# Attention into SwiGLU on one core: regrouping the feed-forward work and re-pricing the planner

## The chip, the cores and the metric

One core of a Trainium2 chip runs the whole program. The metric is the device time of one execution in microseconds, lower is better; the time before is the median of three runs.

## The reference

Attention with a threshold on 8 batches of 8 heads, 576 rows and 64 columns per head, and a SwiGLU feed-forward on the 4608 rows that come out of it.

```
scores = (1/8) * q @ k.T                       # per batch and head, 576 x 576
thresh = max(scores, axis=-1) - tau            # tau = 0.02
scores = where(scores >= thresh, scores, -1e9)
attn   = softmax(scores);  o = attn @ v        # 576 x 64 per head
x  = o of all heads side by side               # 4608 x 512
xn = x / sqrt(mean(x*x) + 1e-6) * rms_g
out = (silu(xn @ w_gate) * (xn @ w_val)) @ w_out   # 512 -> 1536 -> 512
```

## The kernel before

The 4608 rows are cut into 36 **chunks** of 128 rows. A chunk `("m", b, c)` holds 128 of the first 512 rows of batch b; a chunk `("v", i, 0)` holds the last 64 rows of batch 2i and of batch 2i+1. The order of the chunks is: four "m" of batch 0, one "v", four "m" of batch 1, four of batch 2, "v", and so on. A chunk takes four **steps**, one for each pair of heads, so there are 144 steps, numbered 0 to 143 here.

A step s does the following.

- A **score burst** on PE (`emit_s`, L377, or L389 for "v" chunks): queries against keys in fp32, two heads on the two halves of the array, into the two PSUM tiles `s_ps`. The next burst needs both tiles read.
- DVE reads them (L410: scale, copy to `ssb`, running minimum to `mx`), POOL adds tau (L417, `nth`), and ACT (L428, L435, L432, L447) with POOL (L461, L466) makes the thresholded weights `wsb`.
- The weights are transposed to `wt`: in the first 16 steps (`N_PE`) by PE (L480) and two DVE copies (L488), later by a DMA on SP's queue (L494).
- PE multiplies them by v (`emit_av`, L511, or L516 for "v" chunks) into `ot`; after two steps DVE divides by the row sums (L537, L538) into `xsb`.

After four steps the chunk is normalized (`emit_x`: ACT L549, POOL L552, L554, L557) and transposed by a DMA on SP (L561) into its place in `xnT[slot]`.

Chunks are put together in **groups** of 1, 2 or 4 (128, 256 or 512 rows) for the feed-forward (`emit_ffn`). For each of 12 slices of the 1536 columns PE does a gate burst of four matmuls (L600) and a value burst of four (L605) into the PSUM `ring`; ACT takes tanh (L614), DVE forms silu (L617) and the product (L622). Then for each chunk an output burst of 12 matmuls (L641), an ACT copy (L647) and a store. A group can start when its last chunk has been transposed.

The program order on each engine is not written by hand. Every piece of work is an `Op` with an engine, an estimated cost in ns (`COST`), dependencies and a priority in units of steps; `order_ops` is a list scheduler that runs through estimated time, always takes the operation that can start first, and among those that can start at the same time the one with the lowest priority number. The result is the order in which each engine's instructions are issued, and on the chip each engine takes them in that order. Feed-forward operations have the priority (step of the group's last chunk + a lag), spread over `pace` steps for each 512 rows (`st`, `dt` and `clock` in `emit_ffn`).

Loads and stores come from SP's queue, loads of v and `w_out` from POOL's. The weights are cast by DVE (L699) as they arrive in the first hundred microseconds.

Of the kernel before, what the change touches and what calls it, by code (L numbers as in the profile page):

```python
# [11 lines left out]
ALU = mybir.AluOpType  # L12

SEM = 160.0
COST = dict(
    s_main=1120.0, s_virt=1130.0, tr4=480.0, tr8=560.0, av_main=360.0, av_virt=500.0, ffn4=216.0,
    ttr=690.0, evac_qk=600.0, evac_kt=350.0, prelu=700.0, exp2=1250.0, exp1=690.0, exp0=690.0,
    mask_d=750.0, mask_g=1740.0, take_g=1300.0,
    trw=560.0, evac_w=420.0, rz=180.0, xmul=400.0, sq=800.0, xn=750.0, pool_tiny=270.0, pool_mean=800.0, pool_dma=800.0, sp=70.0,
# [15 lines left out]
def order_ops(ops, ring_sizes):  # L35


    import heapq

    ring_free = {r: [(0.0, i) for i in range(n)] for r, n in ring_sizes.items()}  # L40
    users = {}
    left = {}
    for i, o in enumerate(ops):
        left[i] = len(o.deps)
        for d in o.deps:
            users.setdefault(id(d), []).append(i)
    pending = {}
    for i, o in enumerate(ops):
        pending.setdefault(o.eng, [])
        if not left[i]:  # L50
            pending[o.eng].append(i)
    eng_free = {e: 0.0 for e in pending}
    dma_free = 0.0
    out = []
    ready_at = {i: 0.0 for i in range(len(ops))}
    while len(out) < len(ops):
        best = None
        for e, lst in pending.items():
            if not lst:
                continue  # L60
            t0 = eng_free[e]
            cand = None
            for i in lst:
                o = ops[i]
                t = max(t0, ready_at[i])
                if o.ring is not None:
                    if len(ring_free[o.ring]) < o.nring:
                        continue
                    t = max(t, sorted(ring_free[o.ring])[o.nring - 1][0])
                k = (t, o.prio, i)  # L70
                if cand is None or k < cand:
                    cand = k
            if cand is not None and (best is None or cand < best[0]):
                best = (cand, e)
        (t, _, i), e = best
        o = ops[i]
        o.start = t
        if o.ring is not None:
            o.slot = []
            for _ in range(o.nring):  # L80
                got = min(ring_free[o.ring])
                ring_free[o.ring].remove(got)
                o.slot.append(got[1])
        eng_free[e] = t + o.cost
        if o.dma:
            dma_free = max(dma_free, t + o.cost) + o.dma
            o.end = max(dma_free, t + o.cost) + 2000.0
        else:
            o.end = t + o.cost
        if o.frees is not None:  # L90
            ring_free["R"].append((o.end + SEM, o.frees[0].slot[o.frees[1]]))
        for slot in o.opens:
            ring_free["R"].append((o.end + SEM, slot))
        pending[e].remove(i)
        out.append(o)
        for j in users.get(id(o), []):
            u = ops[j]
            ready_at[j] = max(ready_at[j], o.end + (0.0 if u.eng == o.eng and not o.dma else SEM))
            left[j] -= 1
            if not left[j]:  # L100
                pending[u.eng].append(j)
    return out
# [3 lines left out]
def kernel(  # L106
# [13 lines left out]
    B, H, S, D = q.shape  # L120
# [51 lines left out]
    NXT = 3  # L172
# [22 lines left out]
    def add(eng, cost, prio, deps, fn, **kw):  # L195
        o = Op(eng, cost, prio, deps, fn, **kw)
        ops.append(o)
        return o


    chunks = []
# [44 lines left out]
    def emit_qk(b, p, prio):  # L246
# [14 lines left out]
        for j in (1, 0):  # L261
# [4 lines left out]

            t = add("PE", COST["tr4"], prio, [los[1 - j], o_id] + last_s.get(("k", b - 2, p), []), tr, ring="R")

# [6 lines left out]

            done.append(add(EVAC[j], COST["evac_qk"], prio, [t], ev, frees=(t, 0)))
        tr_of.append(t)
# [12 lines left out]
    def emit_k_tail(b, prio):  # L290
# [9 lines left out]
        deps = [x for p in range(NP) for x in last_s.get(("k", b - 2, p), [])]  # L300
        t = add("PE", COST["tr4"], prio, [tail_load["k", b], o_id] + deps, tr, ring="R")

        def ev(o):
            nc.scalar.copy(out=kTt[b % 2], in_=ring[t.slot[0]][:, 0:64 * NP].rearrange("p (a n) -> p a n", n=TAIL))

        kt_ready[b] = add("ACT", COST["evac_kt"], prio, [t], ev, frees=(t, 0))
        tail_load.setdefault(("use", i), []).append(t)

    def emit_q_tail(i, prio):
        def tr(o):  # L310
            for p in range(NP):
# [35 lines left out]
    def emit_batch_inputs(b):  # L347
        base = first_step[b - 1] if b else -10
        emit_tail_load(b, base + (4 if b else 1))
        for p in range(NP):  # L350
            pr = base + 3.3 * p + 3 if b else -10 + p
            emit_qk(b, p, pr)
            if p == 0:
                emit_k_tail(b, pr + (2 if b else 0.2))
        emit_v(b, base + 5 if b else -1)
        if b % 2:
            emit_q_tail(b // 2, base + 14.5)
# [305 lines left out]


    ci_of = {c: i for i, c in enumerate(chunks)}
    groups = [[("m", 0, 0), ("m", 0, 1)], [("m", 0, 2), ("m", 0, 3)]]
    for i in range(B // 2):
        if i:
            groups.append([("m", 2 * i, c) for c in range(4)])
        if i % 2:  # L670
            groups.append([("v", i - 1, 0), ("v", i, 0)])
        if 2 * i + 1 < B - 1:
            groups.append([("m", 2 * i + 1, c) for c in range(4)])
    groups += [[("m", B - 1, 0), ("m", B - 1, 1)], [("m", B - 1, 2)], [("m", B - 1, 3)]]
    place, last_of = {}, {}
    for gi, g in enumerate(groups):
        for j, c in enumerate(g):
# [2 lines left out]
    xt_op = {}  # L680
# [7 lines left out]
    n = 0  # L688
# [21 lines left out]
    for j in range(4):  # L710
        o = add("POOL", COST["pool_dma"], W_FROM + W_STEP * n + j, [], lambda o, j=j: nc.gpsimd.dma_start(
            out=wo[:, 3 * j:3 * j + 3], in_=wo_src[:, 3 * j:3 * j + 3]), dma=3000.0)
        wo_ld.append(gated(o, W_FROM + W_STEP * n + j))

    for s, (ci, p) in enumerate(steps):
        kind, b, c = chunks[ci]
        so = s_of[s] = emit_s(s)
        emit_softmax(s, so)
        emit_av(s)
        if p % 2:  # L720
            emit_half(s)
        if p == NP - 1:
            gi, j = place[ci]
            xt_op[ci] = emit_x(ci, s, gi % NXT, 128 * j)
            if ci in last_of:
                g = groups[last_of[ci]]
                emit_ffn(last_of[ci] % NXT, [(ci_of[x], xt_op[ci_of[x]]) for x in g], s + 5, PACE)
            if kind == "v" and 2 * b + 2 < B:
                emit_batch_inputs(2 * b + 2)
            if kind == "m" and b % 2 and c == 3 and b + 2 < B:  # L730
                emit_batch_inputs(b + 2)
# [11 lines left out]
            o.fn(o)  # L743


PACE = 16.0
FIRST = 0
WAYS = ("pg", "pp")
NSTAGE = 4
# [43 lines left out]
```

## Time and profile before

| what | value |
|---|---|
| runs | 639.76, 640.0, 643.23 us; median 640.0 |
| the profiled execution | 637.34 us, of which the span from the first to the last instruction is 635.6 us |
| PE busy | 602.6 us (95%) |
| ACT, DVE, POOL busy | 461.5 us (73%), 441.3 us (69%), 382.3 us (60%) |
| mean granted PE clock | 0.986 |
| bytes moved by DMA | 84.29 MB, 133 GB/s on average |

Busy time of PE counts the pipeline's latency of each burst, so that 95% busy doesn't say that no time is lost; how much work a stretch holds is worked out in the prediction from the distances between starts of bursts that follow each other without a wait.

### The profile page before, as it was taken

The page shows a single profiled execution, that of the slowest core. Times are in us where ns is not written, and L with a number is a line of the kernel's source. Part 1 is how long each engine was busy: PE and PEld are TensorE (multiplying, and loading weights), DVE is VectorE, ACT ScalarE, POOL GpSimd, SP SyncE. Part 2 cuts the span into 40 slices and gives each one's busy share as a digit, 9 for nine tenths or more (in the row PEclk, how much of TensorE's full clock was granted, in tenths as well). Part 3 has the DMA queues.
Part 4 walks back from the last instruction along what each step waited for, and adds up shares of the span by engine and source line. Part 5 has one row for each costly group of instructions (what it writes and reads, how often), then busy time and mean ns, then how long its engine had stood idle before and what let it go on. Part 6 is the DMA issues. An engine that isn't in the chain of part 4 may idle for free.

```text
span 635.6 us, 13838 instructions
## 1 busy us (share of the span) xinstructions
PE 602.6 (95%) x5008; PEld 362.5 (57%) x5008; DVE 441.3 (69%) x1129; ACT 461.5 (73%) x741; POOL 382.3 (60%) x518
## 2 busy tenths in 40 slices
PE   5799979997999999999999999999999999998996
PEld 3566756764645545555765445555555444556774
DVE  3799976756578758865868765886587658856653
ACT  2778857687776878977977777987687877876332
POOL 4799565758495745966785654876396744653000
PEclk9999979999799999999999999999999999999999
DMA  9999876887798556987896549997797553445100
GB/s 167 163 186 175 163 169 116 145 164 125 146 142 119 105 149 138 146 141 152 175 170 121 87 94 185 150 152 134 181 145 133 104 142 82 94 118 117 42 34 35
DMA packets 296725, 84.29 MB, mean 133 GB/s; under 512 B 287440, under 2 KB 288976, under 8 KB 296656
## 3 DMA queue, kind: packets, MB, share of 16 engines
q1 hardware_dynamic: 256400, 77.11, 57.8%
q0 software_dynamic: 40256, 6.30, 13.5%
q8 instruction: 39, 0.64, 0.4%
q14 instruction: 30, 0.25, 0.2%
HBM read 37.75 MB, written 9.44 MB: 74 GB/s over the span
## 4 chain that ended last, share of the span: by engine, by line
PE 79%; DVE 8%; DMA 4%; issue 3%; POOL 3%; ACT 2%; SPq 0%; DVEq 0%; POOLq 0%; ACTq 0%
PE s_ps L377 24%; PE ring L641 12%; PE ring L605 12%; PE ring L600 12%; PE ot L511 6%; PE ring L264 4%; DVE ssb L410 3%; DMA wt<-wsb 3%; PE s_ps L389 2%; PE s_ps L641 2%; PE ot L516 1%; POOL wsb L461 1%; DVE sl L617 1%; DVE hf L622 1%; PE s_ps L600 1%
## 5 line engine op out<-in xcount | busy, mean ns | idle before, releaser
L410 DVE CUSTOM_DVE_ANT_0 ssb<-s_ps,zrow 128x576 f32<-128x576 f32 x288 | 209.5, 753 | 104.1 <-PE s_ps L377 72.3
L428 ACT ACTIVATE ssb<-ssb,nth 128x576 f32<-128x576 f32 x216 | 159.1, 765 | 49.0 <-POOL nth L417 48.4
L377 PE MATMUL s_ps<-qkT 64*128 64x512 f32 x512 | 172.4, 658 | 8.2 <-DVE mx L410 5.7
L461 POOL TENSOR_SCALAR wsb<-ssb,nth 128x576 f16<-128x576 f32 x72 | 124.9, 1735 | 9.4 <-PE ring L480 3.7
L417 POOL TENSOR_SCALAR nth<-mx 128x2 f32<-128x2 f32 x144 | 32.1, 223 | 152.6 <-DVE mx L410 131.1
L605 PE MATMUL ring<-xnT,wv 128*128 128x512 f16 (+2 forms) x520 | 106.9, 328 | 2.1 <-DVE sl L617 2.1
L600 PE MATMUL ring<-xnT,wg 128*128 128x512 f16 (+2 forms) x524 | 107.4, 327 | 0.0
L377 PEld LDWEIGHTS s_ps<-kTt,qkT 64*128 64x128 f32 x512 | 63.8, 192 | 57.2 <-issue 54.9
L466 POOL TENSOR_TENSOR wsb<-wsb,esb 128x576 f16<-128x576 f16 x72 | 92.3, 1281 | 5.6
L614 ACT ACTIVATE th<-ring 128x512 f32<-128x512 f32 (+2 forms) x131 | 63.4, 488 | 35.9 <-PE ring L600 33.2
L435 ACT ACTIVATE wsb<-ssb 128x1152 f16<-128x1152 f32 x72 | 83.7, 1162 | 4.8 <-DMA wt<-wsb 1.5
L617 DVE SCALAR_TENSOR_TENSOR sl<-th,ring 128x512 f32<-128x512 f32 (+2 forms) x131 | 72.3, 552 | 17.8 <-ACT th L614 17.6
L641 PE MATMUL ring<-wo,hf 128*128 128x512 f16 x372 | 84.7, 379 | 0.0
L622 DVE TENSOR_TENSOR hf<-ring,sl 128x512 f16<-128x512 f32 (+2 forms) x130 | 72.9, 561 | 10.7 <-PE ring L605 1.1
L333 POOL DMA_DIRECT2D va<-in_v_dram x112 | 77.2, 694 | 2.7 <-PE s_ps L377 0.6
L377 PEld LDWEIGHTS s_ps<-qkT 64*128 64x128 f32 x512 | 51.1, 189 | 46.9 <-DVE mx L410 24.6
L600 PEld LDWEIGHTS <-wg 128*128 128x128 f16 x624 | 54.6, 98 | 31.8 <-issue 0.5
L605 PEld LDWEIGHTS <-wv 128*128 128x128 f16 x624 | 53.5, 97 | 32.4 <-issue 4.2
L511 PE MATMUL ot<-va,wt 128*128 128x65 f16 x1280 | 62.0, 195 | 5.8 <-DMA wt<-wsb 4.9
L641 PEld LDWEIGHTS <-hf 128*128 128x128 f16 x432 | 40.6, 98 | 47.1 <-issue 1.9
L447 ACT ACTIVATE esb<-ssb,nth 128x576 f16<-128x576 f32 x72 | 55.4, 770 | 15.7 <-POOL nth L417 15.5
L511 PEld LDWEIGHTS <-wt 128*128 128x128 f16 x1280 | 53.1, 98 | 19.3 <-DMA wt<-wsb 6.2
(53 smaller groups left out, 574.6 us busy)
## 6 DMA issues: line engine op xcount, KB each, us to landing
qkn<-in_k_dram SPq DMA_DIRECT2D x64, 128.0 KB, 3.5
qkn<-in_q_dram SPq DMA_DIRECT2D x64, 128.0 KB, 3.4
out_dram<-osb SPq DMA_DIRECT2D x32, 256.0 KB, 2.6
stage<-in_moe_w_gate_dram SPq DMA_DIRECT2D x12, 256.0 KB, 3.2
stage<-in_moe_w_val_dram SPq DMA_DIRECT2D x12, 256.0 KB, 3.5
va<-in_v_dram POOLq DMA_DIRECT2D x80, 32.0 KB, 3.6
va<-in_v_dram POOLq DMA_DIRECT2D x32, 64.0 KB, 4.0
wt<-wsb SPq DMA_TRANSPOSE x128, 3.2
```

What stands on the lines that cost most here:

```text
L377: nc.tensor.matmul(s_ps[h][:, lo:lo + n], qkT[b % 2][p][hs, c], src[hs], start=True, stop=True)
L410: nc.vector.tensor_tensor_reduce(out=ssb[a][:, h], in0=s_ps[h][:, 448:1024], in1=zrow, scale=-1.0 / 8.0, scalar=3.0e38, op0=ALU.add, op1=A ...
L428: nc.scalar.activation(out=ssb[a][:, h], in_=ssb[a][:, h], func=PRELU, scale=-1.0, bias=nth[m][:, h:h + 1], **PRELU_KW)
L435: nc.scalar.activation(out=wsb[s % NW], in_=ssb[a], func=AF.Exp)
L461: nc.gpsimd.tensor_scalar(out=wsb[s % NW][:, h], in0=ssb[a][:, h], scalar1=nth[m][:, h:h + 1], scalar2=None, op0=ALU.is_le)
L466: nc.gpsimd.tensor_tensor(out=wsb[s % NW][:, h], in0=wsb[s % NW][:, h], in1=esb[es], op=ALU.mult)
L511: nc.tensor.matmul(ot[:, cs], w[:, 4 * h + j], va[b % 2][:, p, 5 * h + j], start=(j == 0), stop=(j == 4))
L600: nc.tensor.matmul(ring[o.slot[0]][:, 0:n], wg[d][:, fs], xnT[slot][:, d, 0:n], start=(d == 0), stop=(d == 3))
L605: nc.tensor.matmul(ring[o.slot[0]][:, 0:n], wv[d][:, fs], xnT[slot][:, d, 0:n], start=(d == 0), stop=(d == 3))
L617: nc.vector.scalar_tensor_tensor(out=sl[i][:, 0:n], in0=th[i][:, 0:n], scalar=1.0, in1=ring[g.slot[0]][:, 0:n], op0=ALU.add, op1=ALU.mult)
L622: nc.vector.tensor_tensor(out=hf[hi][:, 0:n], in0=ring[vv.slot[0]][:, 0:n], in1=sl[i][:, 0:n], op=ALU.mult)
L641: nc.tensor.matmul(ring[o.slot[0]], hf[hs[fc][0]][:, 128 * j:128 * (j + 1)], wo[:, fc], start=(fc == 0), stop=(fc == NFC - 1))
```

## The change

The groups are now made of consecutive chunks of either kind, in the sizes 2, 2, 2, 2, then six of 4, then 2, 1, 1. Before they were, in chunks: (0,1), (2,3), (5-8), (9-12), (4,13), (14-17), (18-21), (23-26), (27-30), (22,31), (32,33), (34), (35); now they are (0,1), (2,3), (4,5), (6,7), (8-11), (12-15), (16-19), (20-23), (24-27), (28-31), (32,33), (34), (35). Both have six groups of 4, five of 2 and two of 1. The lag in the priority of a group goes from 5 to 10 steps, the pace from 16 to 13 steps for 512 rows. The estimated cost of a score burst goes from 1120 to 1260 ns ("m") and from 1130 to 1250 ns ("v"). `SLACK` is 0, so that the new line in `order_ops` gives what the old one gave.

```diff
+SLACK = 0.0
 COST = dict(
-    s_main=1120.0, s_virt=1130.0, tr4=480.0, ...
+    s_main=1260.0, s_virt=1250.0, tr4=480.0, ...
...
-            ready_at[j] = max(ready_at[j], o.end + (0.0 if u.eng == o.eng and not o.dma else SEM))
+            wait = 0.0 if u.eng == o.eng and not o.dma else SEM + (SLACK if u.eng == "PE" else 0.0)
+            ready_at[j] = max(ready_at[j], o.end + wait)
...
-    groups = [[("m", 0, 0), ("m", 0, 1)], [("m", 0, 2), ("m", 0, 3)]]
-    for i in range(B // 2):
-        if i:
-            groups.append([("m", 2 * i, c) for c in range(4)])
-        if i % 2:
-            groups.append([("v", i - 1, 0), ("v", i, 0)])
-        if 2 * i + 1 < B - 1:
-            groups.append([("m", 2 * i + 1, c) for c in range(4)])
-    groups += [[("m", B - 1, 0), ("m", B - 1, 1)], [("m", B - 1, 2)], [("m", B - 1, 3)]]
+    groups, at = [], 0
+    for n in SIZES:
+        groups.append(chunks[at:at + n])
+        at += n
+    assert at == len(chunks)
...
-                emit_ffn(last_of[ci] % NXT, [(ci_of[x], xt_op[ci_of[x]]) for x in g], s + 5, PACE)
+                emit_ffn(last_of[ci] % NXT, [(ci_of[x], xt_op[ci_of[x]]) for x in g], s + LAG, PACE)
...
-PACE = 16.0
+PACE = 13.0
+SIZES = (2, 2, 2, 2, 4, 4, 4, 4, 4, 4, 2, 1, 1)
+LAG = 10.0
```

The instructions on each engine are the same in kind, shape and number; only their order moves (lines of the changed kernel from `order_ops` on are two higher, weight casts two lower). Three places show it.

**PE, step 36** (`s_ps` is the score tile, `wt` a transposed weight tile, `ot` its product with v, `wv` and `wg` the value and gate weights). Before, the burst is followed by the first of ten matmuls against v:

```order
L377 MATMUL s_ps_172<-qkT_0_82 128x512
L377 MATMUL s_ps_173<-qkT_0_82 128x512
L377 MATMUL s_ps_172<-kTt_90,qkT_0_82 128x64
L377 MATMUL s_ps_173<-kTt_90,qkT_0_82 128x64
L511 LDWEIGHTS wt_120
L511 MATMUL ot<-va_95,wt_120 128x65
```

In the changed kernel the same burst is followed by a value burst, a gate burst and another value burst of a group of 256 rows, and only then by the matmuls against v:

```order
L379 MATMUL s_ps_172<-qkT_0_82 128x512
L379 MATMUL s_ps_173<-qkT_0_82 128x512
L379 MATMUL s_ps_172<-kTt_90,qkT_0_82 128x64
L379 MATMUL s_ps_173<-kTt_90,qkT_0_82 128x64
L607 LDWEIGHTS wv_70
L607 MATMUL ring_176<-xnT_141,wv_70 128x256
L607 LDWEIGHTS wv_71
L607 MATMUL ring_176<-xnT_141,wv_71 128x256
```

Before, steps 32 to 40 hold no feed-forward burst at all; now each of them holds one to four.

**ACT, steps 50 to 52** (`ssb` scores, `wsb` weights, `th` tanh of a gate burst, `osb` an output row block, `xsq` the sum of squares that starts a chunk's normalization). Before:

```order
L614 ACTIVATE th_144<-ring_175 128x512
L428 ACTIVATE ssb_96<-ssb_96,nth_108 128x576 x2
L435 ACTIVATE wsb_114<-ssb_96 128x1152
L447 ACTIVATE esb_113<-ssb_97,nth_109 128x576
L647 ACTIVATE osb_170<-ring_176 128x512
L428 ACTIVATE ssb_97<-ssb_97,nth_109 128x576
L432 ACTIVATE wsb_115<-ssb_97 128x576
L647 ACTIVATE osb_171<-ring_175 128x512
```

Now:

```order
L649 ACTIVATE osb_171<-ring_177 128x512
L274 COPY qkT_3_89<-ring_175 128x512
L551 ACTIVATE xsq_127,ssq_130<-xsb_126 128x512
L323 COPY qTv_93<-ring_176 128x512
L449 ACTIVATE esb_112<-ssb_98,nth_107 128x576
L430 ACTIVATE ssb_98<-ssb_98,nth_107 128x576
L434 ACTIVATE wsb_116<-ssb_98 128x576
L430 ACTIVATE ssb_96<-ssb_96,nth_108 128x576 x2
L437 ACTIVATE wsb_114<-ssb_96 128x1152
```

Before, a tanh and output blocks of a group stand among the weights of these steps; now the last output block of group (6,7) is copied ahead of them, and the first tanh of group (8-11) comes after three more rows.

**DVE, steps 17 to 19** (L410 reads the scores of a step, L488 copies transposed weights of an earlier step). Before:

```order
L410 ISA ssb_97,mx_100<-s_ps_172,zrow 128x576
L410 ISA mx_100 128x1
L488 COPY wt_121<-ring_177 128x640
L488 COPY wt_121<-ring_175 128x512
L410 ISA ssb_97,mx_100<-s_ps_173,zrow 128x576
L410 ISA mx_100 128x1
L488 COPY wt_117<-ring_176 128x640
L488 COPY wt_117<-ring_177 128x512
```

Now:

```order
L490 COPY wt_121<-ring_176 128x640
L490 COPY wt_121<-ring_175 128x512
L624 TENSOR_TENSOR hf_153<-ring_177,sl_145 128x256
L412 ISA ssb_96,mx_99<-s_ps_172,zrow 128x576
L412 ISA mx_99 128x1
L412 ISA ssb_96,mx_99<-s_ps_173,zrow 128x576
L412 ISA mx_99 128x1
L490 COPY wt_117<-ring_176 128x640
L490 COPY wt_117<-ring_175 128x512
```

The transposed weights of steps 14 and 15 were copied during and after the scores of step 19 (`ssb_97`, `mx_100`); now they are copied before and after those of step 18 (`ssb_96`, `mx_99`).

More of the change, by code (lines that the diff above doesn't have):

```diff
@@ L14 @@
 SEM = 160.0
+SLACK = 0.0
 COST = dict(
-    s_main=1120.0, s_virt=1130.0, tr4=480.0, tr8=560.0, av_main=360.0, av_virt=500.0, ffn4=216.0,
+    s_main=1260.0, s_virt=1250.0, tr4=480.0, tr8=560.0, av_main=360.0, av_virt=500.0, ffn4=216.0,
     ttr=690.0, evac_qk=600.0, evac_kt=350.0, prelu=700.0, exp2=1250.0, exp1=690.0, exp0=690.0,
```

## The prediction

> **What bounds the kernel now.** I read the page first (engine shares and slices), then the windows, then one line's windows, PE's timeline and the waits. On the page:
>
> ```profile
> span 635.6 us, 13838 instructions
> ...
> PE 602.6 (95%) x5008; PEld 362.5 (57%) x5008; DVE 441.3 (69%) x1129; ACT 461.5 (73%) x741; POOL 382.3 (60%) x518
> ...
> PE   5799979997999999999999999999999999998996
> ...
> PEclk9999979999799999999999999999999999999999
> ```
>
> PE is the bound from about 200 us on. The slices that are not full, and the two in which the granted clock dips, lie before. The windows, cut where score bursts 0, 16, 24, 32, 48 and the last one start (columns: stretch, length, then busy time of PE, PEld, DVE, ACT, POOL, then granted clock, DMA share and GB/s):
>
> ```profile
> 9.60:65.50 55.90, 50.53 (x433) 34.50 (x433) 46.97 (x121) 39.70 (x58) 44.35 (x59) 1.00 0.99 178
> 65.50:99.60 34.10, 30.01 (x281) 20.66 (x280) 27.42 (x73) 21.97 (x39) 17.69 (x23) 0.90 0.76 160
> 99.60:141.60 42.00, 41.79 (x395) 28.81 (x394) 27.69 (x78) 32.28 (x58) 27.42 (x36) 1.00 0.80 143
> 141.60:202.20 60.60, 53.88 (x386) 32.44 (x384) 39.75 (x99) 43.74 (x67) 42.62 (x59) 0.92 0.87 135
> 202.20:576.50 374.30, 372.39 (x3024) 206.22 (x3023) 264.41 (x648) 298.89 (x460) 237.98 (x321) 1.00 0.71 134
> 576.50:635.60 59.10, 51.18 (x488) 37.87 (x488) 32.74 (x104) 22.98 (x62) 6.15 (x9) 1.00 0.20 52
> ```
>
> PE's busy time includes latency, so I price its work by distances between starts where nothing waits:
>
> ```profile
> 119.40 0.61 PE L605 MATMUL ring<-xnT,wv 128*128 128x256 f16 x4
> 119.85 0.60 PE L600 MATMUL ring<-xnT,wg 128*128 128x256 f16 x4
> 120.28 0.60 PE L605 MATMUL ring<-xnT,wv 128*128 128x256 f16 x4
> ...
> 218.34 5.18 PE ring L641 x24
> ...
> 390.09 1.02 PE ring L264 x8
> ...
> 404.04 1.13 PE L377 MATMUL s_ps<-qkT 64*128 64x512 f32 x4
> 405.00 0.34 PE L377 MATMUL s_ps<-kTt,qkT 64*128 64x64 f32 x4
> 405.27 1.04 PE L600 MATMUL ring<-xnT,wg 128*128 128x512 f16 x4
> 406.15 0.48 PE L511 MATMUL ot<-va,wt 128*128 128x65 f16 x10
> 406.47 1.02 PE L605 MATMUL ring<-xnT,wv 128*128 128x512 f16 x4
> 407.33 1.03 PE L600 MATMUL ring<-xnT,wg 128*128 128x512 f16 x4
> 408.29 1.13 PE L377 MATMUL s_ps<-qkT 64*128 64x512 f32 x4
> ```
>
> A score burst takes 1.23 us (404.04 to 405.27), a gate or value burst 0.86 at 512 rows and 0.44 at 256, a burst against v 0.32, an output burst 5.18/2 = 2.59, a pair of q and k transposes 1.0. Switching into a score burst costs 0.10 (0.96 against 0.86). With these prices I add up PE's work in any stretch of the program, by counting bursts in the two orders. Over the whole program both come to 560 us; the other 75 us of the span are PE without work, and only they can change.
>
> **Steps 32 to 47, the main term.** The feed-forward gate bursts and the score bursts by stretch (PE, PEld):
>
> ```profile
> 99.60:141.60 42.00, 9.03 (x60) 5.55 (x60) 1.00 0.80 143
> 141.60:166.90 25.30, 0.00 (x0) 0.00 (x0) 0.81 0.86 144
> 166.90:202.20 35.30, 9.20 (x36) 3.29 (x36) 0.99 0.88 129
> ...
> 141.60:166.90 25.30, 15.41 (x65) 9.21 (x65) 0.81 0.86 144
> ```
>
> The first three rows are L600, the last L377. From 141.6 to 166.9 there is no gate burst: group (5-8) has to wait for chunk 8. A score burst has 8 records, so 65 are 8.1 bursts, 3.1 us each, while PE had about 1.8 us of work per step. Here the softmax sets the pace. For steps 32 to 47 before: 16 score bursts (19.7), 15 against v (4.8), 4 pairs of transposes (4.0), 17 feed-forward bursts at 512 rows (14.6) and switches (1.3) make 44.4 us in 60.6 us, 16.2 without work. In the changed order the same steps carry 47 feed-forward bursts at 256 rows (20.7), 4 output bursts (10.4) and one more burst against v: 61.1 us. The idle time is filled with work that is taken from stretches where PE is full (6.4 us from steps 24 to 31, 2.7 from the tail, the rest from later steps), and those shorten by as much. Some idle time remains. Steps 24 to 31, where the order already alternates score and feed-forward bursts of 256 rows, hold 40.5 us of work in 42.0, so 1.5 in 8 steps; I take 3.0 in 16 steps. Gain 13.2; ends: 16.2 (nothing is left idle) and 8.
>
> The clock belongs to this term: 0.81 granted from 141.6 to 166.9, 1.00 where PE is fed. [...]
>
> **Steps 16 to 23.** 34.1 us hold 22.2 us of work before and 21.5 now, at a clock of 0.90. Steps 20 to 22 had no feed-forward burst; now steps 20 and 21 have four and three, of group (0,1), which is running there in both. But DVE, which also casts the weights here, was busy for 27.42 us and does the same work, so the gain is at most 34.1 - 27.4 = 6.7; at worst the same waits return behind other bursts (loss 1). I take 2, nearer to the row of DVE than to none, because DVE waits between its own instructions too.
>
> **Steps 0 to 15.** Work and pieces are the same, but the burst against v now follows three score bursts after its own in steps 5 to 13, where it followed four (six in step 13), and the later score bursts stand behind it in PE's order. Step 8:
>
> ```profile
> 38.42 1.52 PE L377 MATMUL s_ps<-qkT 64*128 64x512 f32 x4
> ...
> 54.08 0.48 PE L511 MATMUL ot<-va,wt 128*128 128x65 f16 x10
> ...
> 32.00:64.00 32.00, 30.58 (x260) 19.90 (x260) 31.02 (x80) 24.75 (x37) 29.82 (x41) 1.00 0.92 178
> ```
>
> That is 15.7 us from its score burst to its burst against v. If this latency stayed, steps would come every 15.7/4 = 3.9 us and not every 3.4 (55.9/16 = 3.5), a loss of about 5 over nine steps. But DVE is at 31.02 of 32 us here: most of the latency is queueing, which shrinks when fewer steps are in flight. I take a loss of 1; ends: gain 1, loss 5.
>
> **Steps 50 to 56: the new dry stretch.** Group (6,7) ends at step 49 with two output bursts, and group (8-11) cannot start before chunk 11 is normalized. Steps 50 to 56 hold 16.9 us of PE work in the new order (29.8 before, inside the full stretch from 202.2): 7 score bursts (8.4), 6 feed-forward bursts (5.2), the rest against v. At the 3.1 us per step seen without feed-forward work they would take 21.7, a loss of 4.8; if the softmax has caught up during the output bursts, none. Before the first gate burst stands 5.2 us of PE work from chunk 11's last burst against v; what has to happen meanwhile is
>
> ```profile
> L538 DVE TENSOR_TENSOR xsb<-ot,rz 128x256 f32<-128x256 f32 x72 | 30.6, 425 | 5.2 <-POOL xn L557 2.7
> L549 ACT ACTIVATE xsq<-xsb 128x512 f16<-128x512 f32 x36 | 22.3, 620 | 2.7 <-DVE xsb L538 2.6
> L554 POOL TENSOR_TENSOR ir<-irm,mhalf 128x1 f32<-128x1 f32 x36 | 21.0, 582 | 3.0
> L557 POOL TENSOR_SCALAR xn<-xsb,ir 128x512 f16<-128x512 f32 x36 | 25.1, 698 | 3.6
> ...
> xnT<-xn SPq DMA_TRANSPOSE x36, 2.5
> ```
>
> 0.4 + 0.6 + 0.6 + 0.7 + 2.5 = 4.8 us and a wait between each two, so the gate burst is late by some 2 us. I take a loss of 3.
>
> **The rest.** From step 57 to the last score burst both orders alternate in the same way and PE is full (372.39 of 374.30): no change, give or take 1. The tail from the last score burst has the same last groups (2, 1, 1); its work goes from 47.8 to 45.1 us (counted above), and its idle time of 11.3 us mostly lies in the groups of one chunk and the last store. The burst against v of step 143 now stands behind two output bursts and will wait less: gain 0.5, ends -1 and 1.5. Grouping, lag, pace and the two costs act through the order alone; `SLACK` of 0 does nothing. Cross-kind groups cost nothing extra on PE: the tail of "v" chunks is stored by the same two DMAs as before, on SP's queue.
>
> **Sum.** 13.2 + 2 - 1 - 3 + 0.5 = 11.7 us. The span falls from 635.6 to 623.9, the profiled execution from 637.3 to 625.6. That execution was 2.7 us below the median of the runs; against the median the forecast is 640.0 - 11.7 = 628.3 us.
>
> **Rivals.** (a) The idle time of steps 32 to 47 is due to the transposing DMAs, not to missing work, and stays.
>
> ```profile
> 151.46 4.29 DMA wt<-wsb
> ...
> 179.57 6.93 DMA wt<-wsb
> ...
> PE ot L511 <- DMA wt<-wsb: 3.2, 3, 2.0
> DVE ssb L410 <- PE s_ps L377: 17.2, 15, 2.5
> ```
>
> For it: those two pieces of the chain, with a DMA share of 0.87. Against it: PE waited for them 3.2 us in three waits, and DVE waited 17.2 us for scores, so the loop was short of PE's order and not of transposes alone; and now 10 to 17 us of work stand between a score burst and its burst against v in steps 32 to 47, where there were 6 to 10 in steps 32 to 39. If 8 more of the 16.2 us stay: 636. [...]
>
> (b) Slower: the shorter reach in steps 5 to 20. If the latencies stay as they were (15.7 us in step 8, and more after step 12 while weights are cast), each burst against v holds back the score burst after the next three. Chaining them by the new order puts step 28 some 16 us later; with 13.2 + 2 - 3 + 0.5 gained elsewhere this gives 643, and it decides the sign from about 13 us of loss. Against it: DVE's 97% says that the queue, not the reach, set the pace.
>
> (c) More is won: nothing remains idle in steps 32 to 47, steps 16 to 23 gain 5, the dry stretch costs nothing: 640.0 - 22 = 618, between 616 and 622.
>
> (d) The reordering moves idle time without removing it, since the work is equal: within 3 us of 640.
>
> **Chances.** Forecast (622 to 633) 0.64, (c) 0.12, (a) 0.13 (633 to 639), (d) 0.06, (b) 0.05. The bound between a change and none is 0.5%, 3.2 us, which is also about what runs of this kernel can tell. Faster takes the forecast, (c) and half of (a): 0.83; same the other half and most of (d): 0.11; slower (b) and a little of (d): 0.06. The range leaves out (b), (d) and half of (c): 619 to 637.
>
> **What would show it.** Right: the granted clock at 1.00 from step 24 on, steps 32 to 47 taking about 64 us with gate bursts throughout, some 3 us of idle PE near step 52, the tail after the last score burst near 56 us. Wrong: PE waiting for transposes or for `mx` in steps 32 to 47, step 16 starting clearly later than 65.5 us, or new idle time of over 5 us after step 57.

## The result, and the profile after

The changed kernel takes 622.96 us (median of four runs, 620.76 to 625.11). The kernel before, in runs beside it, takes 639.88. The ratio is 0.973 with a 95% interval of 0.967 to 0.979, a gain of 16.9 us where 11.7 were forecast. The profiled execution took 620.76 us.

The page of the changed kernel, the lines that answer to those of before:

```profile
span 619.0 us, 13823 instructions
...
PE 592.0 (96%) x5008; PEld 354.8 (57%) x5008; DVE 439.2 (71%) x1129; ACT 460.0 (74%) x741; POOL 383.6 (62%) x518
...
PE   5798999999999999999999999999999999999996
...
PEclk9999999999999999999999999999999999999999
```

Both dips of the granted clock are gone in this execution, and of the gaps in PE's row only those of the first 60 us and of the end are left. The windows of the changed kernel, cut at the same six places (starts of score bursts 0, 16, 24, 32, 48 and 143; columns as before):

```profile
9.30:68.40 59.10, 51.73 (x452) 35.13 (x452) 48.97 (x127) 40.39 (x60) 45.32 (x60) 1.00 0.98 180
68.40:96.80 28.40, 25.73 (x277) 17.55 (x276) 23.78 (x66) 21.79 (x36) 17.57 (x21) 1.00 0.93 159
96.80:131.70 34.90, 34.90 (x329) 25.67 (x328) 26.62 (x76) 27.50 (x50) 24.87 (x34) 1.00 0.88 158
131.70:195.80 64.10, 63.27 (x562) 43.39 (x561) 46.81 (x131) 50.88 (x91) 42.90 (x57) 1.00 0.87 143
195.80:562.60 366.80, 365.78 (x2947) 198.73 (x2946) 264.33 (x639) 297.02 (x453) 241.25 (x326) 1.00 0.75 136
562.60:619.00 56.40, 47.82 (x437) 32.44 (x436) 26.36 (x84) 20.55 (x54) 5.62 (x9) 0.98 0.20 58
```

Steps 32 to 47 (the fourth row) take longer than before, 64.1 us against 60.6, because they now hold 61.2 us of work; the clock there went from 0.92 to 1.00. The gate bursts (L602 is L600 of before) in these steps and in steps 48 to 56:

```profile
131.70:195.80 64.10, 13.90 (x93) 8.54 (x92) 1.00 0.87 143
195.80:228.00 32.20, 3.72 (x16) 1.24 (x16) 1.00 0.74 126
```

93 records are 23 gate bursts of 256 rows where the first eight of these steps had none. What one such step looks like now, in PE's timeline of the changed kernel:

```profile
147.47 1.13 PE L379 MATMUL s_ps<-qkT 64*128 64x512 f32 x4
148.44 0.33 PE L379 MATMUL s_ps<-kTt,qkT 64*128 64x64 f32 x4
148.70 0.61 PE L607 MATMUL ring<-xnT,wv 128*128 128x256 f16 x4
149.22 0.60 PE L602 MATMUL ring<-xnT,wg 128*128 128x256 f16 x4
149.90 1.37 PE L379 MATMUL s_ps<-qkT 64*128 64x512 f32 x3
150.86 0.33 PE L379 MATMUL s_ps<-kTt,qkT 64*128 64x64 f32 x2
151.11 0.59 PE L379 MATMUL s_ps<-qkT 64*128 64x512 f32 x1
```

The feed-forward bursts (from 148.70 on) stand between the score bursts at 147.47 and 149.90; DVE reads the scores of the first of the two from 149.09 to 150.52.

To see where the 16.6 us between the two spans came from, each stretch's time less PE's work in it, priced with the distances of the prediction, gives PE's time without work, called idle here (us). It contains what PE lost to a low clock, since the prices were read where the granted clock was 1.00 (99.6 to 141.6 and 202.2 to 576.5 us of the kernel before). The work in the table adds up to 558.4 in both kernels; with the transposes ahead of step 0 it is some 560.

| steps | before: time, work, idle | after: time, work, idle | idle won |
|---|---|---|---|
| 0 to 15 | 56.0, 39.0, 17.0 | 59.0, 39.8, 19.2 | -2.2 |
| 16 to 23 | 34.1, 22.2, 11.8 | 28.4, 21.5, 7.0 | 4.8 |
| 24 to 31 | 42.0, 40.5, 1.4 | 34.9, 34.1, 0.8 | 0.6 |
| 32 to 47 | 60.6, 44.4, 16.2 | 64.0, 61.2, 2.9 | 13.3 |
| 48 to 56 | 38.0, 37.4, 0.6 | 32.3, 27.7, 4.5 | -3.9 |
| 57 to 142 | 336.2, 327.1, 9.0 | 334.6, 329.0, 5.5 | 3.5 |
| 143 to the end | 59.1, 47.8, 11.3 | 56.4, 45.1, 11.3 | 0.0 |

The last column adds up to 16.1; the first score burst also starts 0.3 us earlier, and the rest is rounding.

### The profile page after: what moved, and what is told of

Read it like the earlier page. It is cut to its first block, busy times and chain, and to the rows that moved or that the text cites. A ratio compares the mean times of both kernels' runs of the same rounds, so it can differ in the third digit from the quotient of the medians.

```text
span 619.0 us, 13823 instructions
## 1 busy us (share of the span) xinstructions
PE 592.0 (96%) x5008; PEld 354.8 (57%) x5008; DVE 439.2 (71%) x1129; ACT 460.0 (74%) x741; POOL 383.6 (62%) x518
## 4 chain that ended last, share of the span: by engine, by line
PE 69%; POOL 9%; DVE 7%; issue 5%; ACT 5%; DMA 3%; SPq 1%; DVEq 0%; POOLq 0%; ACTq 0%
PE s_ps L379 21%; PE ring L602 12%; PE ring L607 11%; PE ring L643 10%; PE ot L513 5%; PE ring L266 4%; POOL wsb L463 3%; POOL wsb L468 3%; PE s_ps L643 2%; DVE ssb L412 2%; PE s_ps L391 2%; DMA wt<-wsb 2%; DVE hf L624 2%; DVE sl L619 2%; DMA qkn<-in_q_dram 1%
## 5 line engine op out<-in xcount | busy, mean ns | idle before, releaser
L412 DVE CUSTOM_DVE_ANT_0 ssb<-s_ps,zrow 128x576 f32<-128x576 f32 x288 | 209.0, 753 | 75.7 <-PE s_ps L379 64.1
L379 PE MATMUL s_ps<-qkT 64*128 64x512 f32 x512 | 161.3, 645 | 4.7 <-ACT qkT L274 2.5
L602 PE MATMUL ring<-xnT,wg 128*128 128x512 f16 (+2 forms) x544 | 110.4, 325 | 1.9 <-DVE hf L624 1.0
L607 PE MATMUL ring<-xnT,wv 128*128 128x512 f16 (+2 forms) x540 | 109.5, 325 | 0.3 <-DVE sl L619 0.2
L619 DVE SCALAR_TENSOR_TENSOR sl<-th,ring 128x512 f32<-128x512 f32 (+2 forms) x136 | 74.4, 547 | 30.8 <-ACT th L616 30.0
L379 PEld LDWEIGHTS s_ps<-kTt,qkT 64*128 64x128 f32 x512 | 59.8, 188 | 55.1 <-issue 52.5
L616 ACT ACTIVATE th<-ring 128x512 f32<-128x512 f32 (+2 forms) x136 | 64.9, 483 | 30.7 <-PE ring L602 29.7
L624 DVE TENSOR_TENSOR hf<-ring,sl 128x512 f16<-128x512 f32 (+2 forms) x135 | 74.7, 553 | 8.9 <-PE ring L607 0.2
L643 PE MATMUL ring<-wo,hf 128*128 128x512 f16 x348 | 79.3, 379 | 0.0
L602 PEld LDWEIGHTS <-wg 128*128 128x128 f16 x624 | 54.3, 98 | 31.2 <-issue 2.4
L379 PEld LDWEIGHTS s_ps<-qkT 64*128 64x128 f32 x512 | 46.7, 185 | 41.6 <-DVE mx L412 16.9
L449 ACT ACTIVATE esb<-ssb,nth 128x576 f16<-128x576 f32 x72 | 55.4, 770 | 15.7 <-POOL nth L419 15.3
```

The lines of the kernel that those rows point to most:

```text
L379: nc.tensor.matmul(s_ps[h][:, lo:lo + n], qkT[b % 2][p][hs, c], src[hs], start=True, stop=True)
L412: nc.vector.tensor_tensor_reduce(out=ssb[a][:, h], in0=s_ps[h][:, 448:1024], in1=zrow, scale=-1.0 / 8.0, scalar=3.0e38, op0=ALU.add, op1=A ...
L602: nc.tensor.matmul(ring[o.slot[0]][:, 0:n], wg[d][:, fs], xnT[slot][:, d, 0:n], start=(d == 0), stop=(d == 3))
L607: nc.tensor.matmul(ring[o.slot[0]][:, 0:n], wv[d][:, fs], xnT[slot][:, d, 0:n], start=(d == 0), stop=(d == 3))
L619: nc.vector.scalar_tensor_tensor(out=sl[i][:, 0:n], in0=th[i][:, 0:n], scalar=1.0, in1=ring[g.slot[0]][:, 0:n], op0=ALU.add, op1=ALU.mult)
L624: nc.vector.tensor_tensor(out=hf[hi][:, 0:n], in0=ring[vv.slot[0]][:, 0:n], in1=sl[i][:, 0:n], op=ALU.mult)
```

## The experiments

Each compares PE's time without work, worked out in the same way from that kernel's own order and trace. The times of all:

| kernel | median us | ratio to before (95%) | idle 0-15 | 16-23 | 24-31 | 32-47 | 48-56 | 57-142 | end |
|---|---|---|---|---|---|---|---|---|---|
| before | 639.88 | | 17.0 | 11.8 | 1.4 | 16.2 | 0.6 | 9.0 | 11.3 |
| changed | 622.96 | 0.973 (0.967-0.979) | 19.2 | 7.0 | 0.8 | 2.9 | 4.5 | 5.5 | 11.3 |
| 1 groups of before | 629.47 | 0.986 (0.980-0.992) | 21.1 | 6.5 | 1.1 | 17.0 | 0.5 | 8.3 | 6.4 |
| 2 new groups only | 634.04 | 0.991 (0.988-0.994) | 17.0 | 11.8 | 1.4 | 3.2 | 11.4 | 13.3 | 6.6 |
| 3 costs of before | 625.17 | 0.979 (0.974-0.984) | 16.4 | 6.8 | 3.3 | 3.3 | 9.6 | 11.3 | 7.1 |
| 4 lag 5 | 641.91 | 1.005 (1.002-1.008) | 20.3 | 6.5 | 0.4 | 2.9 | 7.4 | 23.7 | 8.6 |
| 6 lag 14 | 621.21 | 0.968 (0.965-0.972) | 21.1 | 7.1 | 2.5 | 2.9 | 0.6 | 10.0 | 8.1 |
| 7 pairs only | 624.56 | 0.975 (0.971-0.980) | 19.5 | 7.0 | 0.7 | 3.3 | 1.8 | 13.4 | 6.7 |
| 8 lag 14, costs of before | 627.31 | 0.978 (0.973-0.983) | 17.0 | 6.1 | 3.7 | 2.7 | 1.6 | 19.0 | 6.8 |
| 9 new costs only | 636.97 | 0.994 (0.992-0.997) | 19.6 | 6.1 | 1.5 | 16.7 | 1.2 | 14.0 | 8.4 |
| 10 old cost to step 15 | 623.08 | 0.974 (0.972-0.976) | 17.0 | 7.4 | 4.3 | 2.2 | 4.4 | 5.5 | 10.8 |
| 11 the same, lag 13 | 623.12 | 0.974 (0.972-0.976) | 17.0 | 6.4 | 4.5 | 2.5 | 0.4 | 16.1 | 6.6 |
| 12 changed, again | 622.92 | 0.973 (0.971-0.975) | 20.8 | 7.0 | 0.8 | 3.0 | 4.3 | 5.5 | 13.3 |

Number 5 adds useless work and stands below by itself; the experiments follow by what they ask, not by number. The idle times are those of one profiled execution, the medians those of all runs. The changed kernel stands in the table twice, in its first row and as number 12: its idle times in the start and at the end differ by 1.6 and 2.0 us from one execution to another.

**1. The groups of before in the changed kernel.** Lag, pace and costs stay new; only the five lines that fill `groups` are the old ones.

```diff
-    for n in SIZES:
-        groups.append(chunks[at:at + n])
-        at += n
+    groups = [[("m", 0, 0), ("m", 0, 1)], [("m", 0, 2), ("m", 0, 3)]]
+    for i in range(B // 2):
...
```

> The changed kernel with the groups of before (lag 10, pace 13 and the new costs kept). Theory 'missing work' (PE loses time where steps hold no feed-forward burst, about 3.1 us per step against 1.7 us of work): steps 33 to 41 are dry again, so steps 32 to 47 (44.0 us of work) again take about 60 us, 16 idle where the changed kernel has 2.9; the 4 us lost at steps 50 to 56 come back as a gain; two dry steps at 110 to 113 cost 1 to 2. About 634 us. Rival 'better prices' (the planner's new score cost, lag and pace make a better order everywhere and the grouping is secondary): within 4 us of 623.

Measured: 629.47 us. The windows of steps 32 to 39 and 40 to 47 of this kernel, all work and then the gate bursts alone:

```profile
134.00:167.00 33.00, 29.73 (x185) 18.93 (x183) 14.83 (x42) 21.83 (x32) 18.17 (x24) 0.74 0.70 131
167.00:194.90 27.90, 27.31 (x201) 15.54 (x200) 20.72 (x53) 23.04 (x36) 23.57 (x34) 1.00 1.09 167
...
134.00:167.00 33.00, 0.00 (x0) 0.00 (x0) 0.74 0.70 131
```

No gate burst in the first eight steps, the clock down to 0.74, and 17.0 us without work as before (16.2). Without the pairs of chunks 4 to 7 there is nothing to fill these steps with, at a lag of 5 or of 10. The whole kernel lost 6.5 us, between the 11 of the expectation and the 4 at most of its rival; its tail was idle for 6.4 us and not 11.3, which the expectation had not foreseen. The place is shown; the tail is a difference of the order that no run isolates.

**5. Useless work in the empty steps of the kernel before.** Three bursts of four matmuls of 256 columns of zeros follow the scores in steps 20 to 22 and 32 to 41. Their product is never read.

```diff
+        if s in WARM:
+            for _ in range(3):
+                def warm(o):
+                    for _ in range(4):
+                        nc.tensor.matmul(ring[o.slot[0]][:, 0:256], id16, zrow[:, 0:256], ...)
+                wo_ = add("PE", 440.0, s + 0.9, [so], warm, ring="R")
...
+WARM = set(range(20, 23)) | set(range(32, 42))
```

> The kernel before, with useless bursts of 4 matmuls of 256 columns (zeros, result not read; 0.44 us each) put on PE in steps 20 to 22 and 32 to 41, three for each step, 17.5 us in all; the order of everything else is nearly that of before. Theory 'missing work': the added bursts fit into PE's idle time there and the softmax loop still sets the pace, so the time stays within 3 us of 639, with the granted clock at 1.00 in these steps. Rival 'cold clock': what the feed-forward bursts bring in the changed kernel is mostly that they keep PE's clock up (0.90 in steps 16 to 23, 0.81 in steps 32 to 39), so useless bursts bring 5 to 8 us too: 631 to 634.

Measured: 636.49 us, ratio 0.993 (0.991 to 0.996). Its windows, steps 16 to 23, 32 to 39 and 40 to 47:

```profile
66.10:101.60 35.50, 33.19 (x348) 22.91 (x347) 28.33 (x78) 23.84 (x41) 18.91 (x25) 0.95 0.76 159
140.60:166.00 25.40, 25.40 (x242) 19.23 (x239) 14.60 (x42) 18.23 (x26) 17.31 (x24) 1.00 0.82 140
166.00:199.30 33.30, 33.30 (x277) 20.56 (x276) 24.93 (x58) 26.12 (x42) 24.32 (x34) 1.00 0.79 138
```

and the window of steps 32 to 39 of the kernel before, then one step of its PE timeline:

```profile
141.60:166.90 25.30, 20.74 (x136) 14.11 (x135) 13.87 (x39) 17.63 (x26) 15.61 (x22) 0.81 0.86 144
...
146.40 1.37 PE L377 MATMUL s_ps<-qkT 64*128 64x512 f32 x3 [0.28 <-DVE mx L410]
...
149.08 1.37 PE L377 MATMUL s_ps<-qkT 64*128 64x512 f32 x3 [0.71 <-DVE mx L410]
```

against one step of the kernel with the filler:

```profile
147.46 1.13 PE L377 MATMUL s_ps<-qkT 64*128 64x512 f32 x4
148.43 0.33 PE L377 MATMUL s_ps<-kTt,qkT 64*128 64x64 f32 x4
148.69 1.48 PE L722 MATMUL ring<-zrow,id 128*128 128x256 f16 x12
150.11 1.31 PE L377 MATMUL s_ps<-qkT 64*128 64x512 f32 x4
```

From score burst to score burst it is 2.68 us without and 2.65 us with 1.4 us of extra work, and the eight steps take 25.3 and 25.4 us. So some 11 us of work (96 matmuls, 24 bursts at 0.44) found room there: the softmax loop set the pace, and PE had the time to give. That the two times agree doesn't mean that the clock made no difference. Cut where step 37 starts, the eight steps are, first in the kernel before, then with the filler:

```profile
141.58:156.22 14.64, 11.03 (x92) 7.62 (x89) 8.95 (x25) 9.92 (x16) 12.11 (x18) 1.00 0.74 119
156.22:166.90 10.68, 9.72 (x49) 6.51 (x47) 4.92 (x14) 7.74 (x11) 3.50 (x5) 0.55 1.02 178
...
140.63:155.89 15.26, 15.26 (x141) 11.29 (x139) 8.71 (x24) 10.11 (x16) 11.87 (x17) 1.00 0.80 125
155.89:165.95 10.06, 10.06 (x100) 7.89 (x99) 5.87 (x18) 8.09 (x11) 5.39 (x7) 1.00 0.85 161
```

In the kernel before, steps 32 to 36 ran at the full clock and were idle all the same: 14.6 us for 8.7 us of work (five score bursts, four against v, a pair of transposes, switches). The low clock came after them, so it did not make the idleness. With the filler these five steps are 0.6 us longer. Steps 37 to 39, at a clock of 0.55 before, are 0.6 us shorter with the filler, although they hold more work; from the score burst of step 39 to the burst behind it there are 2.33 us before (163.54 to 165.87, at a granted clock of 0.50) and 1.23 with the filler (162.98 to 164.21, at 1.00). So the low clock did cost time in these three steps, and the time that the extra work cost in the five hid it. How much the clock costs by itself no run shows, because PE is full with the filler (25.40 of 25.40 us).

Over the whole program the run is 4.0 us faster than before (interval 2.8 to 6.0); 636.49 lies inside the expectation's 3 us around 639 and above the rival's 631 to 634. In the profiled executions the spans are 635.5 and 635.6: steps 16 to 56 take 170.6 us against 174.6, and steps 57 to 142, whose instructions stand in the same order on every engine in both, take 339.7 against 336.2. The filler, with a mean granted clock of 0.997 against 0.986 in these two executions, is thus worth some 4 of the change's 16.9 us by this run; what the clock has of that isn't told apart from small shifts of the order around the filler and from what the filler itself cost.

**2. The new groups alone.** Costs, lag and pace as before.

```diff
-    s_main=1260.0, s_virt=1250.0, ...
+    s_main=1120.0, s_virt=1130.0, ...
-PACE = 13.0
+PACE = 16.0
-LAG = 10.0
+LAG = 5.0
```

> Only the new groups; costs, lag 5 and pace 16 of before. Theory 'missing work': steps 46 to 52 (about 12 us of work in 7 steps) and 83 to 85 are dry and cost some 10 and 4 us at 3.1 us per step, steps 20 to 22 stay without feed-forward work as before (11.8 idle in steps 16 to 23 against 7.0), steps 0 to 15 keep the reach of before (gain 2). About 634 us. Rival 'grouping is all': 621 to 625. Rival 'better prices': 637 to 641.

Measured: 634.04 us, as expected. Steps 32 to 47 are filled (3.2 us idle), but the pairs are used up too early and steps 46 to 52 run dry: 11.4 us idle in steps 48 to 56. The windows of steps 46 to 51 and 52 to 56:

```profile
202.50:219.50 17.00, 13.98 (x111) 9.06 (x111) 9.80 (x30) 12.16 (x19) 13.07 (x19) 0.99 0.73 138
219.50:244.40 24.90, 24.58 (x200) 11.79 (x200) 16.39 (x40) 17.55 (x28) 13.53 (x19) 0.80 0.49 99
```

**4. The changed kernel with a lag of 5.** `LAG = 5.0`, nothing else.

> The changed kernel with the old lag of 5 steps. PE's work is the same, but each group's bursts are ordered so early that the next group is not there when they end: steps 45 to 52, 65 to 67, 81 to 84, 97 to 100, 113 to 116 and 129 to 131 hold no feed-forward burst. Theory 'missing work': 26 dry steps at 3.1 us against about 1.7 us of work cost some 30 us, less the 4 of the one dry stretch now: about 647 us. Rival 'work is work' (a full buffer of output bursts ahead of each dry stretch lets the softmax run ahead, so that dry steps cost nothing): 620 to 626.

Measured: 641.91 us, 1.005 (1.002 to 1.008): the new groups, the new pace and the new costs with the old lag lose all that was gained. The work is the same. But every group is finished before the next can start, and 26 steps from step 45 to 131 stand in the order with no feed-forward burst. They are idle for 23.0 us, 0.9 each. The expectation had put some 30 us on them and came out 5 us too high. So the gain is not made by the work or its pieces, but by spreading it over all the steps, and grouping and lag have to do it together. The pace was not changed alone in any run.

**6. A lag of 14.** `LAG = 14.0`.

> The changed kernel with a lag of 14 steps and not 10: the bursts of group (6,7) are spread until chunk 11 is ready, so no step from 24 to 76 is dry; 51.7 us of PE work (and not 45.1) come after the last score burst, taken from steps that stay full. Theory 'missing work': the 4.5 us of idle time at steps 48 to 56 go to about 0.5, nothing else changes: 619, 4 us below the changed kernel. Rival 'the late work costs': the longer tail adds idle time (11.3 us after the last score burst now) and eats the gain: 622 to 626.

Measured: 621.21 us. The dry stretch is gone as expected (0.6 us idle in steps 48 to 56, where the changed kernel has 4.5), but 1.7 came back in steps 24 to 31 and 4.5 after step 57. Its interval (0.965 to 0.972) touches that of the changed kernel run again (0.971 to 0.975), and the two were not timed on one chip: a small gain is possible, not shown.

**7. Pairs throughout.** `SIZES = (2,) * 17 + (1, 1)`.

> The changed kernel with all groups of two chunks (17 of 2, then 1, 1): no dry step at all after step 22, and 2.1 us more PE work for the many more switches; DVE and ACT get more, shorter operations on 256 columns. Theory 'missing work': -4 and +2 against the changed kernel, 621. Rival 'short operations': gate and product on DVE take 0.415 + 0.424 us for 256 columns against 0.684 + 0.690 for 512, so twelve pairs of slices for each of six former groups add 72 x 0.30 = 22 us to DVE's 439, and PE waits for it where bursts alternate fast: 628 or more.

Measured: 624.56 us. Dry steps go (1.8 us), the tail shortens, but PE has 2.1 us more work, and 13.4 us stand idle in steps 57 to 142. It did not get the 621 of its expectation, nor the 628 of the rival.

**3. The old costs in the changed kernel.** `s_main=1120.0, s_virt=1130.0`.

> The changed kernel with the old costs of a score burst (1120 and 1130 ns) in the planner. Theory 'missing work': steps 22 to 24 and 49 to 52 are dry (loss 2 and 2 more than now), steps 0 to 15 have the old reach of four score bursts (idle 17.0 and not 19.2, gain 2). About 625 us. Rival 'better prices': 631 or more.

Measured: 625.17 us. The price that the planner puts on a score burst sets how many score bursts stand between a step's scores and its product with v: with the old price four in steps 5 to 13, with the new one three. Idle time in steps 0 to 15 falls from 19.2 to 16.4 us with the old price, and more comes back later (9.6 against 4.5 in steps 48 to 56, 11.3 against 5.5 after). The rival's 631 or more did not come; the interval (0.974 to 0.984) overlaps that of the changed kernel (0.967 to 0.979), so that a loss by the old price is possible, not shown.

**9. The new costs in the kernel before.** The same line, the other way round.

> The kernel before with the new costs of a score burst alone (1260 and 1250 ns); groups, lag 5 and pace 16 of before. Theory 'missing work plus matched prices': steps 30 to 41 stay dry, so some 14 of the 16 us idle of steps 32 to 47 stay; the scattered waits from step 57 to 142 (9.0 us before, 5.5 in the changed kernel, 11.3 with the old costs in it) shrink by 3 to 5; the start gets the shorter reach and loses 2. About 637 us. Rival 'the costs do nothing alone': 640.

Measured: 636.97 us, as expected, but not by the steps expected. Steps 16 to 23 are down to 6.1 us of idle time from 11.8, so here the costs alone bring what the lag and the pace bring in run 3 (6.8); the two ways don't add up (7.0 with both). But the scattered waits after step 57, which the new costs were expected to clear, grew from 9.0 to 14.0 us. That theory falls.

**8. A lag of 14 with the old costs.**

> The changed kernel with a lag of 14 steps and the old costs of a score burst: steps 5 to 13 keep the reach of four score bursts (idle time of steps 0 to 15 was 16.4 with the old costs and 19.2 with the new), no stretch is dry but pairs of steps at 65, 73 and one each at 97, 109, 126. Theory 'missing work': -2.8 for the start, -4 for steps 48 to 56, +2 for the single dry steps against the changed kernel: 618. Rival 'better prices': the new costs are worth more than the start loses: 623 to 627.

Measured: 627.31 us, some 9 above the expectation and at the upper end of the rival's 623 to 627. The two gains that were to add up are there (17.0 us in steps 0 to 15 and 1.6 in steps 48 to 56), and 19.0 us of idle time in steps 57 to 142 eats them.

**10. The old cost of a score burst in steps 0 to 15 only.**

```diff
-        o = add("PE", COST["s_main" if kind == "m" else "s_virt"], s, deps, fn)
+        o = add("PE", (1120.0 if s < 16 else COST["s_main" if ...]), s, deps, fn)
```

> The changed kernel with a score burst priced 1120 ns in steps 0 to 15 only. From step 57 on PE's order holds the same work step by step as the changed kernel. Steps 5 to 13 have the reach of four score bursts again; steps 22 to 24 become dry. If the reach of three is what costs steps 0 to 15 their 19.2 us of idle time (17.0 before): these steps fall to 16.5 to 17, the dry steps cost 2, together 622 to 623. If not: 625.

Measured: 623.08 us, against 622.92 for the changed kernel on the same chip. The window of steps 0 to 15:

```profile
9.70:65.70 56.00, 50.95 (x434) 34.85 (x434) 47.03 (x121) 39.80 (x58) 44.41 (x59) 1.00 0.98 178
```

The reach of four brings the start back to 56.0 us, exactly as before. But work for steps 22 to 24 is missing then, and steps 24 to 31 are idle for 4.3 us instead of 0.8: the 2 to 3 us move there.

**11. The same with a lag of 13.** The version that the runs before it pointed to: the old start and no dry stretch.

> Score bursts priced 1120 ns in steps 0 to 15 and 1260/1250 later, lag 13, pace 13, the new groups. No stretch of steps is dry from 25 on (single steps at 84, 100, 109, 113 and 129), the start has the reach of four. Theory: against the changed kernel -2.5 for the start, -4 for steps 48 to 56, +2 for steps 23 and 24 and the single dry steps, and the tail's idle time as in the other runs with a lag above 10 (7 to 8 us, not 11.3): 615 to 618. Rival 'idle time only moves' (as with a lag of 14, where the dry stretch went and the time fell by 2 us at most): 620 to 623.

Measured: 623.12 us. The rival held: idle time only moved. Steps 48 to 56 are down to 0.4 and the tail to 6.6 us, but steps 24 to 31 have 4.5 and steps 57 to 142 have 16.1. What weight loads on PE wait for from step 57 on, in this kernel (line waited for: us, times, longest):

```profile
PEld L513 <- DMA wt<-wsb: 7.6, 11, 1.2
PEld s_ps L379 <- DVE mx L412: 5.7, 13, 1.0
...
PEld L602 <- DMA xnT<-xn: 1.7, 1, 1.7
```

and in the kernel before:

```profile
PEld s_ps L377 <- DVE mx L410: 7.8, 21, 0.4
...
PEld L511 <- DMA wt<-wsb: 2.2, 2, 1.5
```

In the same stretch of the changed kernel no wait for a transposed tile `wt` shows, neither for a weight load nor for a matmul; in run 8 it is 4.8 us and in run 9 5.6 us. So part of the scattered time is PE arriving at a product with v whose transpose is still under way.

**12. The changed kernel once more**, beside runs 9 to 11.

> The changed kernel as it is, beside the others on the same chip: 621 to 624.

Measured: 622.92 us. From step 57 to 142 its idle time is 5.5 us again, and in each eight steps within 0.1 us of the first profile, as in run 10, whose instructions stand in the same order there. What differs between two executions is the start (19.2 and 20.8 us) and the tail (11.3 and 13.3). The mean granted clock of this execution is 0.990, of the first profile 0.998; in the start of this one it is 0.50 from 51.4 to 58.2 us, where the first profile has 1.00.

## Why the prediction was right, and where it was not

The main term was right in mechanism and size. The total fits less well: 622.96 lies one us above the lower end of the stated range (622 to 633), and the gain was 5.2 us larger than forecast. Steps 16 to 23 gave 2.8 us more and the steps from 57 on 3.5 us more than was put down for them; the other terms took some of that back. That the errors left the total inside the range is in part luck. Rival (c), 616 to 622, was missed by one us, with one of its three conditions met (nearly 5 won in steps 16 to 23). Rival (d), within 3 us of 640, falls by the 16.9 us.

**Steps 32 to 47: right, in size too.** Forecast a gain of 13.2, measured 13.3 (16.2 to 2.9 us). The stretch takes 64.1 us where "about 64" was said. In all the kernels without the groups of before it has 2.2 to 3.3 us of idle time, in all those with them and without filler 16.2 to 17.0, whatever the lag and costs. Run 5 shows the reason that the prediction gave, a loop that left PE without work, at the full clock too (steps 32 to 36). That the clock's loss lies inside the 16.2 us follows from how they are counted; how large it is stays open, since run 5 doesn't isolate it.

**Rival (a), the transposes, falls.** Three lines of the waits in steps 32 to 47 of the changed kernel, one each of weight loads, matmuls and DVE:

```profile
PEld L513 <- DMA wt<-wsb: 1.2, 2, 0.9
...
PE ot L513 <- DMA wt<-wsb: 0.4, 1, 0.4
...
DVE ssb L412 <- PE s_ps L379: 2.9, 6, 1.2
```

The matmuls' waits for transposes went from 3.2 to 0.4 us and DVE's waits for scores from 17.2 to 2.9, with the same transposes and the same DMA share of 0.87. In the timeline of the changed kernel above whole bursts start in program order. Inside a score burst the matmuls don't always. In the burst at 149.90 the matmuls of 64 columns of the first head (150.86) start before the last record of the 512-column matmul of the second head (151.11), which stands ahead of them in the program; the first weight load of that matmul (150.57) came after a wait of 0.38 us for DVE, whose read of its tile ended at 150.52. In step 36, whose order is shown with the change, the added bursts stand before the product with v and not behind it.

**The dry stretch: 3 taken, 3.9 measured.** The prediction had the first gate burst of group (8-11) late by some 2 us, because chunk 11 has to be normalized and transposed first. The changed kernel there, PE's timeline from chunk 11's last burst against v on, the issue of the transpose, and the weight loads of the gate burst:

```profile
206.67 0.48 PE L513 MATMUL ot<-va,wt 128*128 128x65 f16 x10
...
210.35 1.20 SPq L563 DMA_TRANSPOSE xnT<-xn  x1
...
211.24 0.49 PE L513 MATMUL ot<-va,wt 128*128 128x65 f16 x10
212.22 1.25 PE L391 MATMUL s_ps<-qkT,qTv 64*64 64x512 f32 x5 [0.48 <-ACT ssb L430]
...
213.71 0.30 PE L391 MATMUL s_ps<-kTt,qTv 64*64 64x64 f32 x6
214.13 1.04 PE L602 MATMUL ring<-xnT,wg 128*128 128x512 f16 x4
...
214.13 0.55 PEld L602 LDWEIGHTS <-wg 128*128 128x128 f16 x4 [0.25 <-DMA xnT<-xn]
```

The gate burst starts 7.5 us after the burst at 206.67, with 5.2 us of work between: 2.3 us late, about as forecast. But PE does not stand before the gate burst for that long: its weight load waits for the transposed chunk for 0.25 us only. Most of the time goes in front of and inside score bursts (the 0.98 us from 211.24 to 212.22 against 0.32 of work), which have to wait until DVE has read their tiles (those of the burst at 209.34 are read from 211.30 to 212.75). The bracket at 212.22 names ACT because its instruction ended last; what the burst needs from ACT, the copied queries `qTv`, was there at 209.6. So the chunk came last, if only by 0.25 us, and up to there the step of the prediction held: the time that PE spent waiting for the tiles it would for the most part have spent waiting for the chunk. What the prediction left out comes behind the gate burst: the loop still makes PE wait for 1.0 and 0.8 us in steps 54 and 55.

**Steps 0 to 15: 1 taken, 2.2 measured.** From score burst to product with v, step 8 of the changed kernel:

```profile
38.86 1.49 PE L379 MATMUL s_ps<-qkT 64*128 64x512 f32 x3
...
51.90 0.49 PE L513 MATMUL ot<-va,wt 128*128 128x65 f16 x10
...
32.00:64.00 32.00, 28.69 (x270) 19.23 (x269) 30.13 (x79) 22.13 (x33) 27.74 (x37) 1.00 0.85 164
```

The latency shrank as argued, from 15.7 to 13.0 us, since fewer steps were queued on DVE, but DVE is then no longer full (30.13 of 32 us against 31.02). Steps come every 59.1/16 = 3.7 us, before every 3.5. Step 16 starts at 68.40, which the prediction had named as a sign of being wrong ("clearly later than 65.5 us"), and in this term it was. Runs 3, 8 and 10 show the cause: with the old price and so the reach of four, idle time there is 16.4 to 17.0; in all the kernels with the new price it is 19.2 to 21.1. Rival (b) is the same mechanism with the latency left as it was; it fell because the latency followed.

**Steps 16 to 23: 2 taken, 4.8 measured.** The bound of 6.7 that DVE's busy time gave was nearer than the value chosen. DVE was busy for 23.78 us of 28.40, less than the 27.42 of before, in 66 instructions against 73: the stretch starts 2.9 us later and holds less of DVE's work, where the prediction assumed the same.

**The rest: 0 taken, 3.5 measured; the term furthest off.** "PE is full, no change" was read from a busy share of 372.39 in 374.30, which counts latency. By work there were 9.0 us to win or lose in 86 steps, and the orders tried spread from 5.5 to 23.7. The changed order happens to have the fewest. Not the costs alone (run 9: 14.0), nor the groups alone (run 2: 13.3), nor the groups with a longer lag (run 6: 10.0) do it. For the changed order the figure came back in runs 10 and 12. But the order alone does not set it: in run 5 the instructions of steps 57 to 142 stand as in the kernel before, and the stretch took 3.5 us longer. So 3.5 of the 16.9 us come from a term that this change did not set out from, no single part of it explains, and it is no larger than what one and the same order can differ by. Why it is the least here stays open.

**Tail: 0.5 taken, none measured** (11.3 us idle in both). Other orders have 6.4 to 8.6 there; what makes the difference was not tried.

## What to carry to other kernels

Price the bound engine's work by distances between starts in full stretches, and subtract it from the time stretch by stretch: PE was 95% busy by the page while 67 of the 626 us from the first score burst on held no work, and the largest hole showed at once. Such a hole is filled only if work is ready there: the size of the groups makes it ready, the lag keeps it from being used up too early, and the groups alone gave 5.5 us (0.991 of 640), the lag, pace and costs without them 9, and the new groups with the old lag lost 3. Where the idle time left is under 2% and scattered, turning the planner's numbers moves it about; mixes whose gains were added up on paper came out 5 to 9 us above it (runs 8 and 11).

## What of the hardware was not expected

The changed order repeats to a tenth of a microsecond: 86 steps with the same instruction order had the same idle time in each eight steps in three executions (runs 10 and 12 and the first profile), while the first 16 steps and the tail of the two profiles of the changed kernel differed by 1.6 and 2.0 us. That isn't so for every order: the kernel before and run 5 share the order of steps 57 to 142 and took 336.2 and 339.7 us for them.

And a low clock can be hidden by the test for it. Useless work brought the clock of steps 32 to 39 from 0.81 to 1.00 and left them at 25.4 us, but only because the five steps at full clock became 0.6 us longer and the three at 0.55 became 0.6 us shorter. The sum over eight steps shows neither.
